# A row transform cut into two 64-row halves, in a kernel that adds a spectral filter and a gated mixture of experts

## The chip, the cores and the metric

The kernel runs on one core of one Trainium2 chip. The metric is the device time of one execution in microseconds (us); lower is better. Engines are named as in the profile: PE is TensorE (PEld its weight loads), DVE VectorE, ACT ScalarE, POOL GpSimd, SP SyncE, which issues most DMAs.

## The reference

```python
x = A_x                                  # [1, 2048, 512] f32
xn = _layernorm(x, axis=-1)
X = rfft2(xn) * (w_r + 1j * w_i)         # over tokens (2048) and features (512)
a = irfft2(X, s=(2048, 512))
gates = softmax(xn @ wg)                 # 8 experts, all 8 used: cw = gates / sum(gates)
h = gelu(einsum("nd,edf->nef", xn, w1))  # f = 1792
b = einsum("ne,ned->nd", cw, einsum("nef,efd->ned", h, w2))
return x + a + b
```

## The kernel before, in words

Nearly all of the time is the mixture of experts. Its two products are done in 32-bit floats split into a high and a low part (`split`: ACT writes the high part, DVE or POOL the low part), so each product is three passes of matmuls (`PASSES`). After a first slice that is done plainly (`mm1`, line 503, and `mm2`, line 525), the rest runs by a scheme of seven products for a two-by-two block (line 931), from about 155 us to the end.

The forward transform of the filter stands in the first stage, between those plain products. The 2048 tokens are 16 groups of 128, group b holding the tokens 16a + b. For each group, in the order `SEQ`:

- `folds` (POOL): sums and differences of the two halves of the feature axis, into `v`.
- `take_u`: `split` of `v` into `u`. `store_u` stores one half of `u` to DRAM as the table T3 of the later scheme, for groups 8 to 15.
- `over_d` (PE, line 360): the transform over features, two outputs p = 0 (even frequencies) and p = 1 (odd), of 268 and 264 columns. Their last 8 columns are the gate logits, for which `gate_tables` put `wg` beside the tables.
- `take_d`: the result becomes `X`, high part by ACT (line 372), low part by DVE (line 376); the gate columns are added into `lg` (lines 378, 380).
- `negate` (ACT, line 384): writes the negated real part behind the imaginary one, so that one matmul reads (real, imaginary) or (imaginary, minus real).
- `over_a` (PE, line 394): the transform over the 128 tokens of the group, 12 matmuls of 128 rows, 128 weight columns and 260 or 256 columns, from tables `mb` that `load_mb` and `split_mb` bring in.
- `take_a` (ACT) copies the result to `ys`, `store_a` (SP) stores it, one DMA for each p.

What runs when is written out by hand. The first stage is 28 blocks of 12 plain matmuls; around each block two numbered slots of `phase_a` are run, 56 in all. Slot 2n comes right behind block n in PE's order, then the ACT and DVE work on the block's result (`hidden`), then slot 2n + 1. `FFT` gives the slot of each group, `LAG` the distance of its steps, `RANK` the order within a slot; `MEANS`, `ROWS`, `SUMS`, `GATES`, `SPREAD` place the rest. `FIRST` is the order of the start, before block 0: loads, layer norm of the first four groups, their transposes (line 228), and matmuls on idle data (`fill`, `fill_rows`) that keep TensorE active. Every engine works in its order. PSUM has eight banks: two for `p1` (blocks of `mm1`, and the gate transposes of `spread`, line 320), four for `psf` (transposes and transforms), two for `p2` (`mm2`).

When a group of four token groups is through `take_d`, `softmax` makes the gates on DVE and ACT, `spread` transposes them and stores them to `cwd`, and `weights_of` reads them back.

## Time and profile before

| | us |
|---|---|
| median of 3 runs | 2265.36 (2263.53 to 2266.42) |
| the profiled execution | 2264.42 |
| its span, first to last instruction | 2262.6 |
| outside the span (2264.42 - 2262.6) | 1.8 |
| stretch with the forward transform | 22 to 135 |

The profile is one execution: the times of single instructions come from it, the medians from others. Instructions on TensorE are pipelined: a matmul's record is longer than the distance to the next one's start, so the net time of a block is read from start to start.

### The profile page before, as it was taken

Reading aid. Unit: us, or ns where it says so; the run is one execution under the profiler, and the core shown is the slowest. Engines: PE = TensorE matmul, PEld = TensorE weight load, DVE = VectorE, ACT = ScalarE, POOL = GpSimd, SP = SyncE. Lnnn points to the kernel's source line nnn. Section 1 sums busy time; section 2 is a strip of 40 time slices with the busy share of each in tenths; the row PEclk is TensorE's granted clock in tenths of the full one; section 3 lists DMA queues with packets and bytes.
Section 4 is the critical chain, followed back from the end, with each engine's and each line's share of the span. In section 5 each row is a group of like instructions: output and inputs, shape, how many; then the busy total and the mean of one; then the engine's idle time right before and its main releaser. Section 6 shows DMA issues by size and latency. Waiting matters only on the chain.

```text
span 2262.6 us, 27515 instructions
## 1 busy us (share of the span) xinstructions
PE 2249.3 (99%) x10271; PEld 1872.0 (83%) x10271; DVE 1891.8 (84%) x1823; ACT 1164.4 (51%) x1559; POOL 961.6 (42%) x660
## 2 busy tenths in 40 slices
PE   9999999999999999999999999999999999999999
PEld 8877888888888888888888888888888888888887
DVE  7758788888888888888878898888898888888776
ACT  7855455445455545545554545454554545455452
POOL 4216353455354544434344444445454434444340
PEclk9999999999999999999999999999999999999999
DMA  5788767677666666666677667766666666766663
GB/s 190 245 274 286 295 231 300 241 286 262 250 237 235 230 249 242 239 247 240 251 259 256 231 224 256 261 244 239 234 232 246 234 246 231 273 228 249 239 237 133
DMA packets 111686, 553.31 MB, mean 245 GB/s; under 512 B 11905, under 2 KB 22273, under 8 KB 55585
## 3 DMA queue, kind: packets, MB, share of 16 engines
q1 hardware_dynamic: 98816, 482.42, 58.5%
q10 hardware_dynamic: 11872, 64.94, 8.0%
q0 software_dynamic: 864, 4.19, 1.0%
q8 instruction: 82, 1.34, 0.2%
q14 instruction: 52, 0.42, 0.1%
HBM read 528.34 MB, written 29.98 MB: 247 GB/s over the span
## 4 chain that ended last, share of the span: by engine, by line
PE 96%; DMA 2%; ACT 1%; DVE 1%; issue 0%; SPq 0%; POOL 0%; ACTq 0%; DVEq 0%
PE pq L931 45%; PE pz L931 45%; PE p L525 1%; PE p L503 1%; PE pq L863 1%; PE psf L360 1%; PE psf L394 1%; DMA xr<-xs_b 1%; PE pq L876 0%; DMA xs_T<-d 0%; DMA mf<-in_mb 0%; DMA cwt<-cwd 0%; DMA acc<-in_x 0%; PE psf L228 0%; DMA cwd<-c 0%
## 5 line engine op out<-in xcount | busy, mean ns | idle before, releaser
L931 PE MATMUL pq<-xr,us 128*128 128x512 f32 x2580 | 619.9, 389 | 0.4 <-issue 0.4
L931 PE MATMUL pz<-hs,vs 128*128 128x512 f32 x2562 | 616.2, 389 | 0.0
L931 PEld LDWEIGHTS pq<-xr,us 128*128 128x128 f32 x2580 | 484.1, 188 | 101.8 <-issue 0.8
L931 PEld LDWEIGHTS pz<-hs,vs 128*128 128x128 f32 x2562 | 479.8, 188 | 99.2
L931 PE MATMUL pz<-hs,va 128*128 128x512 f32 x1974 | 473.7, 389 | 0.0
L931 PE MATMUL pq<-xr,ua 128*128 128x512 f32 x1932 | 464.3, 389 | 1.6 <-DMA xr<-xs_b 1.1
L931 PEld LDWEIGHTS pz<-hs,va 128*128 128x128 f32 x1974 | 369.4, 188 | 75.7
L931 PEld LDWEIGHTS pq<-xr,ua 128*128 128x128 f32 x1932 | 362.5, 188 | 77.7 <-DMA xr<-xs_b 1.6
L188 ACT CAST hs<-c 128x1024 fp32r<-128x1024 f32 x213 | 223.1, 1047 | 368.8 <-DVE c L1041 306.0
L1057 DVE TENSOR_TENSOR acc<-pz,acc 128x1024 f32<-128x1024 f32 x318 | 386.4, 1215 | 29.8 <-PE pz L931 28.5
L191 DVE TENSOR_TENSOR hs<-c,hs 128x1024 fp32r<-128x1024 f32 x213 | 302.5, 1420 | 78.9 <-ACT hs L188 78.9
L191 POOL TENSOR_TENSOR va<-raw,va 128x512 fp32r<-128x512 f32 x81 | 126.4, 1560 | 488.2 <-ACT va L188 477.6
L191 POOL TENSOR_TENSOR ua<-raw,ua 128x512 fp32r<-128x512 f32 x78 | 136.5, 1750 | 277.9 <-ACT ua L188 277.9
L1022 DVE TENSOR_TENSOR hs<-c,hs 128x1024 fp32r<-128x1024 f32 x162 | 211.5, 1305 | 48.9 <-ACT hs L1025 48.9
L1025 ACT CAST hs<-c 128x1024 fp32r<-128x1024 f32 x162 | 170.7, 1053 | 120.5 <-PE pz L931 64.3
L965 DVE TENSOR_TENSOR c<-pq,cwb 128x1024 f32<-128x1024 f32 x162 | 197.1, 1217 | 3.1 <-ACT pq L990 3.1
L191 POOL TENSOR_TENSOR us<-raw,us 128x512 fp32r<-128x512 f32 x52 | 73.4, 1411 | 184.1 <-ACT us L188 184.1
L996 ACT ACTIVATE c<-c 128x1024 f32<-128x1024 f32 x54 | 57.3, 1061 | 160.7 <-DVE c L995 160.7
L191 POOL TENSOR_TENSOR vs<-raw,vs 128x512 fp32r<-128x512 f32 x55 | 78.2, 1421 | 111.9 <-ACT vs L188 111.9
L995 DVE TENSOR_TENSOR c<-pq,c 128x1024 f32<-128x1024 f32 x54 | 66.1, 1224 | 64.3 <-PE pq L931 64.3
L1001 ACT ACTIVATE pq<-pq 128x1024 f32<-128x1024 f32 x54 | 54.4, 1008 | 125.2 <-DVE pq L1000 125.2
L1000 DVE TENSOR_TENSOR pq<-pq,c 128x1024 f32<-128x1024 f32 x54 | 66.5, 1232 | 62.1 <-PE pq L931 62.1
(185 smaller groups left out, 2448.5 us busy)
## 6 DMA issues: line engine op xcount, KB each, us to landing
xr<-xs_T SPq DMA_DIRECT2D x215, 1024.0 KB, 4.8
xr<-xs_b SPq DMA_DIRECT2D x161, 1024.0 KB, 4.8
cwb<-cwd SPq DMA_DIRECT2D x124, 256.0 KB, 5.3
raw<-in_wb ACTq DMA_DIRECT2D x27, 1024.0 KB, 4.9
raw<-in_wa ACTq DMA_DIRECT2D x26, 1024.0 KB, 5.0
xr<-cbd SPq DMA_DIRECT2D x32, 384.0 KB, 5.2
xs_b<-x SPq DMA_DIRECT2D x6, 1024.0 KB, 5.9
xs_T<-d SPq DMA_DIRECT2D x12, 512.0 KB, 4.9
```

Of the source, the lines that this page charges most:

```text
L188: nc.scalar.copy(dst[:, 0], src)
L191: (eng or nc.vector).tensor_tensor(dst[:, 1], src, r32(dst[:, 0]), op=ALU.subtract)
L360: nc.tensor.matmul(px, u[:, p, hu, k, :], fds[p][:, h, k, :R2], start=(n == 0), stop=(n == 5))
L931: nc.tensor.matmul(pt[:, m, :], w[:, hw, k, m * P : (m + 1) * P], x[:, hx, k, :], start=(start and n == 0), stop=(n == 5), skip_group_chec ...
L965: nc.vector.tensor_mul(dst, src, g)
L995: nc.vector.tensor_add(self.h22, self.X, self.h22)
L996: nc.scalar.activation(self.h22, self.h22, AF.Gelu_apprx_tanh)
L1000: nc.vector.tensor_add(self.X, self.X, self.u2)
L1001: nc.scalar.activation(self.X, self.X, AF.Gelu_apprx_tanh)
L1022: (nc.vector if self.u else eng(LOW["u0"][k - 4])).tensor_tensor(t[:, 1], h, r32(t[:, 0]), op=ALU.subtract)
L1025: nc.scalar.copy(t[:, 0], h)
L1057: nc.vector.tensor_add(to, self.z[(0, 1, 0, 1, 4, 4, 5)[k]], to)
```

## The change

The transform over the 128 tokens of a group is done as its first step says it can be: the sum and the difference of the two halves of 64 tokens, then a transform of 64 on each, which give the even and the odd frequencies. `folds` takes sum and difference on POOL (two more instructions for each group, a new tile `w`), so rows 0 to 63 of what `over_d` writes carry the sums and rows 64 to 127 the differences. `over_a` then runs pairs of matmuls of 64 rows, one on the upper and one on the lower half of the array, into two PSUM banks; real and imaginary part of the output lie in the two halves of the 128 weight columns, and one matmul covers both p (258 columns). `negate` and `store_u` go: the sign is in the table `mb` (192 instead of 256 columns), and T3 is split from `w` in `folds`, with two tiles `d` that `sums` uses too. `take_d` writes both p into one tile `X`. `store_a` issues four DMAs for a group instead of two, each of 64 partitions. The gate logits come out as sums and differences, so `softmax` first multiplies them by a table `pair` on TensorE, through a `p1` bank. `fill_rows` changes from 12 matmuls of 64 rows and 256 columns to 4 of the whole array and 16 of 64 rows, all of 128 columns. In `FIRST` one `fill` of a single matmul goes and one of two becomes one of one; the scale of group 3 moves from ACT to DVE, a weight's low part from DVE to POOL. Slots, ranks and engines of other steps are set anew, among them the moments of two token groups from slot 0 to slots 2 and 3, and the gate transposes of the first four groups from slot 17 to 15.

```diff
-XC = 144
+XC = 272
-XB = 2
+XB = 1
-MEANS = (0, 0, 0, 0, 8, 9, 5, 5, 29, 25, 27, 28)
+MEANS = (0, 0, 3, 2, 8, 9, 5, 5, 29, 25, 27, 28)
-SPREAD = ((17, 17), (26, 28), (41, 41), (50, 52))
+SPREAD = ((17, 15), (26, 30), (41, 41), (50, 52))
-SCALES = (0, 0, 0, 1)
+SCALES = (0, 0, 0, 0)
...
-    a = np.arange(P)
+    a, h = np.arange(P), np.arange(P // 2)
     m, cb = [], []
     for b in range(NB):
-        th = 2 * np.pi * (((16 * a[:, None] + b) * a[None, :]) % S) / S
-        m.append(np.concatenate([np.cos(th), np.sin(th)], 1))
-        th = th.T
+        th = [2 * np.pi * (((16 * h[:, None] + b) * (2 * h[None, :] + q)) % S) / S for q in range(2)]
+        th = np.concatenate(th, 0)
+        m.append(np.concatenate([np.sin(th), np.cos(th), -np.sin(th)], 1))
+        th = 2 * np.pi * (((16 * a[None, :] + b) * BINS[:, None]) % S) / S
         cb.append(_hl(np.concatenate([-np.sin(th), np.cos(th), np.sin(th)], 1)))
     out["mb"] = np.stack(m)
+    one = np.eye(H)
+    out["pair"] = np.block([[one, one], [one, -one]])
...
     def folds(b):
         g, n = divmod(b, 4)
         a = ags[g][:, :, :, n * P : (n + 1) * P]
+        w = fa.tile([P, 2, 2, P], F32, name="w")
+        nc.gpsimd.tensor_tensor(w[:, 0], a[:, 1], a[:, 0], op=ALU.add)
+        nc.gpsimd.tensor_tensor(w[:, 1], a[:, 1], a[:, 0], op=ALU.subtract)
         v = vs[b] = fa.tile([P, 2, 2, P], F32, name="v", bufs=VB)
-        nc.gpsimd.tensor_tensor(v[:, 0], a[:, 1], a[:, 0], op=ALU.add)
-        nc.gpsimd.tensor_tensor(v[:, 1], a[:, 1], a[:, 0], op=ALU.subtract)
+        nc.gpsimd.tensor_tensor(v[:, :, :, :H], w[:, :, :, :H], w[:, :, :, H:], op=ALU.add)
+        nc.gpsimd.tensor_tensor(v[:, :, :, H:], w[:, :, :, :H], w[:, :, :, H:], op=ALU.subtract)
+        if b >= 8:
+            i, c = divmod(b - 8, 4)
+            t3 = fa.tile([P, 2, TB], F32R, name="d", bufs=2)[:, 0].rearrange("p (h k t) -> p h k t", h=2, k=2)
+            split(t3, w[:, 1], eng(LOW["t3"]))
+            nc.sync.dma_start(xs["T3"][i][:, :, :, c * P : (c + 1) * P], r32(t3))
     def take_u(b):
         u = us[b] = fa.tile([P, 2, 2, 2, P], F32R, name="u", bufs=2)
         split(u.rearrange("p s h k t -> p h s k t"), vs.pop(b), eng(LOW["u"]))
-
-    def store_u(b):
-        if b >= 8:
-            i, c = divmod(b - 8, 4)
-            nc.sync.dma_start(xs["T3"][i][:, :, :, c * P : (c + 1) * P], r32(us[b][:, 1]))
...
     def softmax(t):
-        c = lgs.pop(t)
+        lg = lgs.pop(t)
+        c = xp.tile([P, 4, E], F32, name="sm")
+        pl = ps1.tile([P, TB], F32, name="p1")[:, : 4 * E].rearrange("p (j e) -> p j e", e=E)
+        nc.tensor.matmul(pl, pair, lg, start=True, stop=True)
         mx = xp.tile([P, 16], F32, name="mx", bufs=2)[:, :4]
-        nc.vector.tensor_reduce(mx, c, axis=AX.X, op=ALU.max)
-        nc.vector.tensor_sub(c, c, mx[:, :, None].to_broadcast([P, 4, E]))
+        nc.vector.tensor_reduce(mx, pl, axis=AX.X, op=ALU.max)
+        nc.vector.tensor_sub(c, pl, mx[:, :, None].to_broadcast([P, 4, E]))
...
     def load_mb(b):
-        mbf[b] = fa.tile([P, 2, P], F32, name="mf", bufs=MFB)
-        nc.sync.dma_start(mbf[b], io["mb"][b].rearrange("p (c a) -> p c a", c=2))
+        mbf[b] = fa.tile([P, 3 * H], F32, name="mf", bufs=MFB)
+        nc.sync.dma_start(mbf[b], io["mb"][b])
     def split_mb(b):
-        mbs[b] = fa.tile([P, 2, 2, P], F32R, name="mb", bufs=2)
+        mbs[b] = fa.tile([P, 2, 3 * H], F32R, name="mb", bufs=2)
         split(mbs[b], mbf.pop(b), eng(LOW["mb"]))
...
         lg = lgs[t][:, j]
+        X = Xs[b] = fa.tile([P, 2, 2, XC], F32R, name="X", bufs=XB)
         for p in range(2):
-            R = ROW[p]
-            Xs[b, p] = fa.tile([P, 2, 3, XC], F32R, name="X", bufs=XB)[:, :, :, :R]
-            px = pxs[b, p][:, : 2 * R].rearrange("p (c r) -> p c r", c=2)
-            nc.scalar.copy(Xs[b, p][:, 0, :2], px)
+            px = pxs[b, p][:, : 2 * ROW[p]].rearrange("p (c r) -> p c r", c=2)
+            nc.scalar.copy(X[:, 0, :, AT[p] : AT[p + 1]], px)
         for p in range(2):
             px = pxs.pop((b, p))
             R2 = 2 * ROW[p]
-            nc.vector.tensor_sub(Xs[b, p][:, 1, :2], px[:, :R2].rearrange("p (c r) -> p c r", c=2), r32(Xs[b, p][:, 0, :2]))
+            sl = slice(AT[p], AT[p + 1])
+            nc.vector.tensor_sub(X[:, 1, :, sl], px[:, :R2].rearrange("p (c r) -> p c r", c=2), r32(X[:, 0, :, sl]))
             if p:
                 nc.vector.tensor_add(lg, lg, px[:, R2:])
             else:
                 (nc.vector.tensor_copy if LOW['lg'] else nc.scalar.copy)(lg, px[:, R2:])
-    def negate(b):
+    def over_a(b):
+        mb, X = mbs.pop(b), Xs.pop(b)
+        py = pys[b] = [psf.tile([P, 512], F32, name="psf")[:, : AT[2]] for _ in range(2)]
+        n = 0
+        for c in range(2):
+            for h, hx in PASSES:
+                for q in range(2):
+                    rows = slice(q * H, q * H + H)
+                    nc.tensor.matmul(
+                        py[q], mb[rows, h, (1 - c) * H : (3 - c) * H], X[rows, hx, c, : AT[2]], start=(n == 0), stop=(n == 5)
+                    )
+                n += 1
+
+    yss = {}
+
+    def take_a(b):
+        st = yss[b] = fa.tile([P, 2, AT[2]], F32, name="ys", bufs=2)
+        for q, py in enumerate(pys.pop(b)):
+            nc.scalar.copy(st[:, q], py)
+
+    def store_a(b):
+        st = yss.pop(b)
         for p in range(2):
-            nc.scalar.mul(Xs[b, p][:, :, 2], r32(Xs[b, p][:, :, 0]), -1.0)
-
-    def over_a(b):
-        mb = mbs.pop(b)
-        for p in range(2):
-            X = Xs.pop((b, p))
-            py = pys[b, p] = psf.tile([P, 512], F32, name="psf")[:, : 2 * ROW[p]]
-            n = 0
             for c in range(2):
-                for h, hx in PASSES:
-                    nc.tensor.matmul(py, mb[:, h, c], X[:, hx, c : c + 2], start=(n == 0), stop=(n == 5))
-                    n += 1
-
-    yss = {}
-
-    def take_a(b):
-        for p in range(2):
-            st = yss[b, p] = fa.tile([P, 2, ROW[p]], F32, name=f"ys{p}", bufs=2)
-            nc.scalar.copy(st, pys.pop((b, p)).rearrange("p (c r) -> p c r", c=2))
-
-    def store_a(b):
-        for p in range(2):
-            nc.sync.dma_start(yd[p][b // 4][:, b % 4], yss.pop((b, p)))
+                to = yd[p][b // 4][:, b % 4, c].rearrange("(q k) r -> k q r", q=2)
+                nc.sync.dma_start(to, st[c * H : c * H + H, :, AT[p] : AT[p + 1]])
...
     def fill_rows(n):
         two = [pt, ps1.tile([P, TB], F32, name="p1")]
+        for _ in range(4):
+            nc.tensor.matmul(pt[:, :P], warm, warm, start=True, stop=True)
         for _ in range(n):
             for h in range(2):
                 rows = warm[64 * h : 64 * h + 64]
-                nc.tensor.matmul(
-                    two[h][:, : 2 * P].rearrange("p (n c) -> p n c", n=2), rows, rows[:, None].to_broadcast([64, 2, P]),
-                    start=True, stop=True,
-                )
+                nc.tensor.matmul(two[h][:, :P], rows, rows, start=True, stop=True)
...
-        fill_rows(6)
+        fill_rows(8)
+    ri = ri[BINS]
```

## Rows read from the trace of the kernel before

**Rows 1.** The page: the span, the busy time of each engine with its share of the span and its instructions.

```profile
span 2262.6 us, 27515 instructions
...
PE 2249.3 (99%) x10271; PEld 1872.0 (83%) x10271; DVE 1891.8 (84%) x1823; ACT 1164.4 (51%) x1559; POOL 961.6 (42%) x660
```

**Rows 2.** Busy time of each engine by stage: the stretch in us from the start of the span, its length, then busy us and instruction count of PE, PEld, DVE, ACT and POOL, the granted clock, the share of the DMA engines and GB/s.

```profile
0.00:25.00 25.00, 20.93 (x121) 17.34 (x122) 20.12 (x43) 16.43 (x36) 12.31 (x26) 1.00 0.80 285
25.00:135.00 110.00, 109.50 (x681) 97.75 (x680) 83.51 (x195) 86.58 (x203) 30.26 (x38) 1.00 0.66 209
135.00:160.00 25.00, 22.14 (x97) 17.20 (x96) 14.31 (x26) 13.65 (x25) 3.19 (x4) 1.00 0.94 303
160.00:2262.60 2102.60, 2096.71 (x9377) 1739.69 (x9375) 1773.84 (x1562) 1047.77 (x1297) 915.81 (x592) 1.00 0.67 245
```

**Rows 3.** Who TensorE waited for, in three stretches one after the other (0 to 30, 30 to 135 and 135 to 210 us): us in total, times, longest.

```profile
PE p L503 <- DVE w L490: 0.8, 2, 0.4
PE p L228 <- ACT u L217: 0.7, 1, 0.7
...
PE psf L394 <- ACT X L384: 0.5, 1, 0.5
...
PE pq L931 <- DVE raw L569: 2.6, 1, 2.6
PE pq L931 <- DMA xr<-xs_b: 1.1, 1, 1.1
```

**Rows 4.** The chain of work that ended last, its first and its last block of line 394: start us, us, what. Each piece is counted to the start of the next, so a block of twelve matmuls appears with its net time. After it, the instructions of line 394 as a whole (ns minimum/median/maximum, first and last start, forms).

```profile
28.08 1.44 PE psf L394 x12
...
133.53 1.43 PE psf L394 x12
...
L394 PEld LDWEIGHTS psf<-X,mb x192: 186/188/193, 27.8 to 134.6; 128*128 128x128 f32 x192
L394 PE MATMUL psf<-X,mb x192: 275/283/387, 27.9 to 134.7; 128*128 128x260 f32 x96, 128*128 128x256 f32 x96
```

**Rows 5.** The warm-up before. First the eleven matmuls of 512 columns on the whole array (line 635: ns minimum/median/maximum, first and last start us), then, in order of time and from narrow windows (each shows what overlaps it), the matmuls of 64 rows and 256 columns behind them, two halves in turn, and weight loads of these.

```profile
L635 PE MATMUL p<-x x11: 628/628/792, 1.5 to 5.9; 128*128 128x512 f32 x11
...
6.47 0.58 PE L644 MATMUL p<-x 64*128 64x256 f32 x2
...
6.85 0.44 PE L644 MATMUL p<-x 64*128 64x256 f32 x4
...
7.13 0.19 PEld L644 LDWEIGHTS p<-x 64*128 64x128 f32 x2
...
7.25 0.19 PEld L644 LDWEIGHTS p<-x 64*128 64x128 f32 x2
```

**Rows 6.** Line 503 between 18 and 24 us: the matmuls of 512 columns (ns minimum/median/maximum), the longest of them those that follow a wait.

```profile
L503 PE MATMUL p<-x,w x17: 283/393/499, 17.8 to 24.0; 128*128 128x512 f32 x14, 128*128 128x256 f32 x3
```

**Rows 7.** TensorE in order of time from 56 to 61 us: a block of line 360, four transposes of 128 columns (line 320), a product.

```profile
56.18 1.62 PE L360 MATMUL psf<-fd,u 128*128 128x268 f32 x12
57.64 0.60 PE L320 MATMUL p<-ident,cw 128*8 128x128 f32 x4
58.00 3.00 PE L503 MATMUL p<-x,w 128*128 128x512 f32 x12
```

**Rows 8.** Groups of ScalarE and then of VectorE between 25 and 135 us, shapes apart: busy us, mean ns of one, idle time before them and what ended it.

```profile
L384 ACT ACTIVATE X<-X 128x260 fp32r<-128x260 f32 x16 | 6.9, 432 | 1.9 <-DVE X L376 1.2 <-DVE mb L191 0.6
L384 ACT ACTIVATE X<-X 128x256 fp32r<-128x256 f32 x16 | 6.7, 419 | 0.0
L188 ACT CAST mb<-mf 128x256 fp32r<-128x256 f32 x15 | 6.2, 415 | 3.9 <-DMA mf<-in_mb 3.9
L188 ACT CAST d<-ag 128x512 fp32r<-128x512 f32 x10 | 6.0, 626 | 2.1 <-DMA xs_T<-d 2.1
...
L191 DVE TENSOR_TENSOR mb<-mf,mb 128x256 fp32r<-128x256 f32 x15 | 6.3, 421 | 2.9 <-ACT mb L188 2.8
```

**Rows 9.** GpSimd folds of line 255 (ns minimum/median/maximum) and, from the order of time, VectorE and GpSimd in the first 21 us: the start of the moments of two token groups, and two low parts of weights while GpSimd folds.

```profile
L255 POOL TENSOR_TENSOR v<-ag x12: 740/752/1003, 31.8 to 117.3; 128x256 f32<-128x256 f32 x12
...
13.77 0.68 DVE L205 BATCH_NORM_STATS2 st<-acc 128x6 f32<-128x512 f32 x1
...
14.58 0.66 DVE L205 BATCH_NORM_STATS2 st<-acc 128x6 f32<-128x512 f32 x1
...
19.11 1.83 DVE L490 TENSOR_TENSOR w<-raw,w 128x256 fp32r<-128x256 f32 x2
...
18.85 0.93 POOL L255 TENSOR_TENSOR v<-acc 128x256 f32<-128x256 f32 x1
```

**Rows 10.** ScalarE in order of time from 56 us: the first instruction after the product that ends at 56.3, and the copy that frees the PSUM buffer of the gate transposes.

```profile
56.54 0.60 ACT L515 ACTIVATE c<-p 128x512 f32<-128x512 f32 x1
...
58.54 0.57 ACT L323 COPY c<-p 8x512 f32<-8x512 f32 x1
```

**Rows 11.** TensorE and VectorE in order of time: the product that runs from 42.15 us, and the last gate sum of the first four token groups.

```profile
42.15 2.95 PE L525 MATMUL p<-h,w 128*128 128x512 f32 x12
...
43.79 0.15 DVE L378 TENSOR_TENSOR lg<-lg,psf 128x8 f32<-128x8 f32 x1
```

**Rows 12.** What the DMA queue of SyncE waited for between 25 and 135 us (us in total, times, longest), and the stores of line 406 as a whole (ns of issue).

```profile
SPq L346 <- DVE mb L191: 36.0, 12, 4.4
...
L406 SPq DMA_DIRECT2D yd<-ys x32: 319/540/1482, 29.2 to 137.9; - x32
```

45 lines of the change are left out of this document (25 added, 20 removed).

## The prediction

> **What bounds the kernel now.** I read the page first: TensorE is busy for 99% of a span of 2262.6 us, VectorE for 84% [rows 1]. That is a mean over stages, so next the busy times by stage [rows 2]. The change touches the first 155 us or so. In the stretch 25 to 135 us, where the forward transform runs, TensorE works 109.5 of 110 us, ScalarE 86.6, VectorE 83.5, GpSimd 30.3. Its waits, third, say the same from the other side [rows 3]: between 30 and 135 us it waits once, 0.5 us, for the negation on line 384. So in this stretch time taken off TensorE is time gained, as long as the other engines keep up. Outside it there are two places with gaps. Before 25 us it is idle for 25 - 20.9 = 4.1 us [rows 2], 0.8 of it in two waits for low parts of weights (line 490), and around 155 us it waits 2.6 us at line 931 [rows 3]. The work behind that second gap starts from the gate transposes that TensorE itself makes in slot 50, so the gap moves with TensorE and I leave it as it is.
>
> **What the change does, part by part.**
>
> *The halves.* Fourth, the chain of waits: a block of line 394 is 12 matmuls in 1.44 us net, the first as the last [rows 4], so 0.120 us each, and with 192 of them 16 blocks and 23.0 us. The new block has again 12 matmuls of 128 weight columns and about as many streamed (258 for 260 and 256), but of 64 rows, in pairs. What a pair costs the trace shows before the change, in the warm-up [rows 5]: there matmuls of 64 rows and 256 columns are issued to the two halves in turn; two loads start at 7.13 us, two at 7.25. A pair takes 0.12 us, what one matmul of 128 rows took. So a block becomes 6 x 0.12 = 0.72 us, and 16 blocks save 11.5 us. If the halves did not run together, nothing would be saved; that is a rival below.
>
> *Going over and back.* Each block stands between matmuls of the whole array, so there are 32 changes between the two forms. Rows 5 show one, while 512 columns still took (5.9 - 1.5) / 10 = 0.44 us, that is with the clock at its lower level of 1.2 GHz. The last whole-array matmul starts at 5.9 us and would be followed at 6.34; the first pair starts at 6.47, 0.13 later. The next pair starts at 6.85, 0.38 behind it, where 256 columns take half of 0.44, 0.22: 0.16 more, the load that could not be hidden behind a running matmul. Together 0.29 at the lower level. At the upper level the load has a price of its own: a matmul after a wait has a record of up to 0.499 us where the median is 0.393 [rows 6], 0.10 more. For the emptying I halve the 0.13 with the clock. That makes 0.165, and 32 x 0.165 = 5.3 us. Bounds: the load alone, 3.2; everything as at the lower level, 9.3. The Trainium skill has the rule: "TensorEngine Tiling (Array Packing)", Key Properties, says that changing the tiling mode drains TensorE, and gives no figure. The 0.13 us agrees with it; by a free change the net gain of this part would be 11.5, by the drain as taken it is 6.2.
>
> *The gate product.* Four matmuls of `pair` with 32 columns in full f32, which the trace of before does not show. The nearest rows are the transposes of 128 columns in f32: four in 0.36 us, from 57.64 to 58.00 [rows 7], 0.09 each. Below, one of these, 0.09; above, all four for one product, 0.36, and a load not hidden, 0.10. I take 0.2, so 0.8 in all (0.4 to 1.8). It waits for the last gate sum of its four groups. For the first four this is done at 43.9 us while a product runs from 42.15 to 44.9 [rows 11], so TensorE need not wait; VectorE, in turn, must now wait for TensorE, about 1 us four times, with its other work queued behind the maximum of line 306.
>
> *The gate transposes of the first four groups.* They take one of the two `p1` banks, now in slot 15, before block 8. Block 8 takes the other, and block 9 needs the first back. It is freed by the copy on line 323, still in slot 17, behind block 8's own gelu and split on ScalarE. Before, block 9 needed only that gelu. The copy ran from 58.54 to 59.1 us, with the gelu at 56.54 right after the product's end [rows 10], while TensorE goes from 56.18 with a transform of about 1.46 us to 57.64 and could start block 9 then [rows 7]: 1.4 us too early. ScalarE's order there is little changed, so I take 1.2 (0 to 1.5).
>
> *The start.* Two moments go from slot 0 to slots 2 and 3, each 0.81 us of VectorE from start to start (13.77 to 14.58) [rows 9], ahead of the two low parts that TensorE waits for at 20 and 21 us. These took 0.95 us each instead of 0.42 (the other low parts of that size, `mb` [rows 8]), while GpSimd was folding [rows 9]. Between the two waits' 0.8 us and the load after each, 1.0 can be won; the 0.7 at the fourth group's transposes [rows 3] I leave, since its scale now queues on VectorE. But GpSimd now folds twice as long there (a fold of 0.75 us, four for a group instead of two [rows 9]). I take -1.0 (-1.3 to +1.0).
>
> *Edits costed at nothing, and their cover.* ScalarE loses 32 negations, 13.6 us, and gains eight high parts for T3 of 0.41 us (the size of `mb`, 0.415 [rows 8]), 3.3 us. VectorE gains eight low parts of 0.42, 3.4 us, and loses a quarter of `mb`, 1.6. GpSimd gains 32 folds of 0.75 us, 24 us on 30. VectorE's instructions beside a fold can be long, as the two above by 0.5 us; I give it 4 us for that. Sum on VectorE: 83.5 + 3.4 - 1.6 + 4 = 89 us of about 105. TensorE covers this, with 16 us to spare; without that cover it is a rival. T3's copies wait on ScalarE for GpSimd, 1.5 us where a fold stands in the slot of its `keep_x` (once), and for `d`, where ScalarE already waits 2.1 us for stores [rows 8]; the freed 10 us cover it. SyncE issues 64 stores instead of 32, 0.54 us each [rows 12], some 17 us more; queued behind them are the loads of `mf`, which wait 36.0 us for their one buffer anyway [rows 12]. The idle-data matmuls of the start stand in TensorE's gaps. `X` in one tile frees as late as the later of its two predecessors did.
>
> **Sum.** -11.5 + 5.3 + 0.8 + 1.2 - 1.0 = -5.2 us. Against the profiled execution, 2264.4: 2259.2. The median of the runs is 0.9 higher, within their 2.9 us, and I leave the 2259.2. A measurement of this kernel tells a change from none from about 0.2% on, 4.5 us.
>
> **Rivals.**
>
> *Dear changes.* At the price of the lower level, 0.29, the sum is -11.5 + 9.3 + 0.8 + 1.2 - 1.0 = -1.2: 2263.2, no change. For it: emptying the array may not halve with the clock. Against: the load's price did nearly (0.16 to 0.10). *Cheap changes*, the load alone and no wait for `p1`: -11.5 + 3.2 + 0.8 - 1.0 = -8.5, 2255.9.
>
> *VectorE becomes the bound.* From 89 of 105 us in the mean it takes only a few places where its work comes in bunches. It decides from the point where TensorE waits 0.7 us more for each of eight groups: 5 us, so -0.2, 2264.2. For it: the new wait for the gate product and twice the folding. Against: the one wait in this stretch [rows 3] was for ScalarE, not VectorE.
>
> *The halves do not run together,* the other side. Twelve loads of 128 columns stay twelve; if one load sets the pace, a block stays at 1.44 us, and the changes come on top: +5.3 + 0.8 + 1.2 - 1.0 = +6.3, 2270.7, slower. It decides from a pair that takes 0.21 us: then the block saves 0.18 us, 2.9 in all, and the rest eats it. For it: the loads' records of 0.19 us exceed the pace of 0.12. Against it: the loads of rows 5 start two at a time. By the Trainium skill, "TensorE: Matmul & The Clock Gate", LDWEIGHTS (loading the stationary operand), a load takes time by its columns and not its rows, which alone would give this rival; the trace agrees as far as a load of 64 rows has the record of one of 128, but shows two at once.
>
> *The clock.* With two idle-data matmuls fewer between 8.7 and 12.4 us the clock could fall to its lower level, where a matmul takes 0.44 for 0.23 us. Over the 7 us of products behind, this costs up to 6, of which the start's gaps hide some: about -5.2 + 4 = -1.2, 2263.2. The granted clock of before is 1.00 in every stage [rows 2].
>
> **How the numbers follow.** Chances: the forecast 0.46; dear changes 0.16; cheap ones 0.16; VectorE 0.11; not together 0.08; the clock 0.03. The forecast counts as faster but for some 0.07 near the bound: faster 0.39 + 0.16 = 0.55. Slower: 0.08, and 0.02 from VectorE. The rest, 0.35, is no change. The range goes from the cheap changes with a better start (-10.5) to the cases around no change and a little over (+2.1): 2254 to 2266.5; what it leaves out is the halves apart and the ends of the other cases.
>
> **What would show it.** In the profile after: blocks of 12 matmuls of 64 rows in about 0.9 us, starting two at a time, with gaps of some 0.1 us ahead of and behind them; four short products of `pair`; a wait of block 9 for line 323; line 490's waits gone; TensorE at line 931 some 5 us sooner. It is wrong if pairs start 0.2 us apart, if the gaps come near 0.3, if TensorE shows waits for VectorE of more than 2 us in the stage, or if line 931 starts sooner and the end does not.

## The result, and the profile after

The changed kernel takes 2283.03 us in the median of four runs (2277.25 to 2285.18), the kernel before 2264.55 beside it: a ratio of 1.0077, 95% interval 1.0056 to 1.0098. It is 18 us slower, outside the predicted range and on the other side of no change. The profiled execution took 2285.18 us, with a span of 2283.4, 20.8 more than before [rows 1].

First the page of the changed kernel, its span and the busy times:

```profile
span 2283.4 us, 27591 instructions
...
PE 2255.0 (99%) x10285; PEld 1869.0 (82%) x10285; DVE 1901.9 (83%) x1835; ACT 1154.3 (51%) x1534; POOL 991.7 (43%) x689
```

Then the busy times by stage, columns as in rows 2:

```profile
0.00:25.00 25.00, 20.86 (x122) 18.02 (x123) 19.44 (x39) 15.02 (x33) 14.06 (x28) 0.93 0.76 278
25.00:135.00 110.00, 98.51 (x616) 80.89 (x615) 87.39 (x187) 71.01 (x165) 58.59 (x67) 0.97 0.61 172
135.00:160.00 25.00, 24.16 (x133) 19.51 (x132) 17.12 (x35) 14.56 (x29) 3.04 (x3) 1.00 0.89 248
160.00:2283.40 2123.40, 2111.49 (x9420) 1750.55 (x9418) 1777.91 (x1576) 1053.72 (x1309) 916.04 (x592) 1.00 0.67 245
```

Between 25 and 135 us TensorE was busy for 109.5 of 110 us [rows 2]; now it is for 98.5, at a mean clock of 0.97, with VectorE at 87.4 (the prediction had 89) and GpSimd at 58.6 for 30.3. Who TensorE waited for, between 30 and 135 and then between 135 and 210 us, tells more than the sums, since before there was one wait of 0.5 us in the first stretch [rows 3]:

```profile
PE psf L403 <- DVE x L256: 3.4, 2, 3.1
PE psf L235 <- DVE xn L226: 2.5, 3, 1.2
PE psf L403 <- DVE lg L393: 2.3, 1, 2.3
PE psf L235 <- ACT ys L413: 1.0, 1, 1.0
...
PE pq L945 <- DVE raw L584: 5.1, 1, 5.1
```

All but one of these name VectorE. Matching the same plain matmul in both traces, the changed kernel is late by 0.6 us at 12 us (times of the kernel before), 2.7 at 70, 9.8 at 91, 13.0 at 140, 15.3 at 155, and 20.9 from 207 us on, and by no more to the end: all of it is lost in the first tenth of the span. Part of it is the clock. Four stretches of the changed kernel, with the same columns:

```profile
8.90:12.30 3.40, 3.17 (x14) 2.99 (x15) 3.27 (x7) 2.32 (x6) 3.20 (x6) 0.52 1.03 415
97.70:104.50 6.80, 5.40 (x20) 4.40 (x21) 4.83 (x12) 4.14 (x11) 4.41 (x6) 0.51 0.75 262
169.40:176.20 6.80, 5.63 (x13) 4.46 (x14) 3.04 (x5) 1.27 (x3) 0.00 (x0) 0.50 1.02 426
224.00:227.40 3.40, 3.40 (x10) 2.67 (x9) 3.40 (x3) 1.32 (x2) 2.95 (x2) 0.51 0.01 5
```

The granted clock is about 0.5 there, the lower of the two levels; before it was 1.00 in every stage [rows 2], though that mean doesn't show the first 6 us, where 512 columns took 0.44 us [rows 5]. TensorE is busy for 17.6 us in these stretches, of which the full clock would have needed half, so up to 8.8 of the 20.8 us are the price of the clock. The last three begin in TensorE's waits of 3.1, 5.1 and 2.0 us, or right behind them. Not every such wait is followed so: behind that of 2.3 us, which ends at 78 us, the clock stayed at 1.00, and so it did in the kernel before behind one of 2.6 us. The second stretch, in order of time (start, us, and the idle time before in brackets):

```profile
99.10 1.66 PE L403 MATMUL psf<-X,mb 64*128 64x258 f32 x11 [3.15 <-DVE x L256]
100.68 4.83 PE L540 MATMUL p<-h,w 128*128 128x512 f32 x12
```

The product behind the wait takes 4.77 us to the next start (105.45) where the other products of line 540 take about 3: this wait of 3.1 us cost some 1.8 more behind it. What VectorE was late with is read one engine further, on ScalarE and then VectorE:

```profile
97.48 0.35 ACT L195 CAST mb<-mf 128x192 fp32r<-128x192 f32 x1 [5.49 <-DMA mf<-in_mb]
97.87 0.36 DVE L198 TENSOR_TENSOR mb<-mf,mb 128x192 fp32r<-128x192 f32 x1 [4.42 <-ACT mb L195]
```

So VectorE itself stood for 4.4 us, at the low part of a table `mb` whose load, issued by SyncE at 89.39 us, came 8 us later; `take_lo` (line 256), whose PSUM bank TensorE needed, stood behind it. SyncE issued the load as soon as its one buffer was free, and 0.9 us behind a load of 1 MB that GpSimd had issued:

```profile
88.48 1.07 POOL L558 DMA_DIRECT2D acc<-in_xt  x1
89.39 0.33 SPq L359 DMA_DIRECT2D mf<-in_mb  x1
```

Both landed between 97.2 and 97.5 us, while in the median a load of `mf` lands 2.4 us after its issue. SyncE's stores of `ys` stand behind it (from 89.77). In the kernel before the two loads were issued together (83.95 and 83.99 us), and the small one had landed by 86.43. So the one buffer puts this load where the large one holds it up; the second half of that is read from the landing times, and no run was made for it.

The waits of 2.3 and 5.1 us have the same look. A little before each, VectorE had stood for a load of gate weights from `cwd`, for 3.0 and 4.0 us:

```profile
72.19 1.67 DVE L555 TENSOR_TENSOR acc<-acc,v 128x1024 f32<-128x1024 f32 x1 [2.97 <-DMA v<-cwd]
...
162.84 0.33 SPq L551 DMA_DIRECT2D cwt<-cwd  x1
...
168.05 0.69 DVE L696 TENSOR_TENSOR acc<-p,cwt 128x512 f32<-128x512 f32 x1 [4.02 <-DMA cwt<-cwd]
```

In the kernel before VectorE waits for no load from `cwd` in this time. The load at 162.84 was issued 7.6 us after ScalarE's store of these gates; before, this took 4.0. Runs below move load and wait together for `mf` and for `cwt`; for `v` it is read from the order of time alone.

Then the queue that the prediction had costed at nothing. What SyncE waited for at the sends of T3 between 20 and 160 us, in the changed kernel (line 271) and, the last line, in the one before (line 265):

```profile
SPq L271 <- DVE d L198: 14.1, 5, 5.3
SPq L271 <- DVE sm L326: 2.5, 1, 2.5
SPq L271 <- DVE sm L320: 1.8, 1, 1.8
SPq L271 <- DVE ag L289: 1.3, 1, 1.3
```

```profile
SPq L265 <- DVE ag L283: 0.4, 1, 0.4
```

Before, `store_u` sent T3 four slots after the folds, when it was long there: 0.4 us of waiting. Now `folds` sends it in its own slot, and SyncE stands for 19.7 us, with the loads behind it. None of the three late loads above stands behind such a send. Where it shows in this trace is at the longest, the send of 110.80 us: behind it `v` is asked for at 117.52 us (101.04 before, some 5 of that more than the kernel is late there anyway), and VectorE stands 1.2 us for it.

### The profile page after: what moved, and what is told of

The parts are those of the page before. It is cut to its first block, busy times and chain, and to the rows that moved or that the text cites. A ratio compares the mean times of both kernels' runs of the same rounds, so it can differ in the third digit from the quotient of the medians.

```text
span 2283.4 us, 27591 instructions
## 1 busy us (share of the span) xinstructions
PE 2255.0 (99%) x10285; PEld 1869.0 (82%) x10285; DVE 1901.9 (83%) x1835; ACT 1154.3 (51%) x1534; POOL 991.7 (43%) x689
## 4 chain that ended last, share of the span: by engine, by line
PE 93%; DVE 3%; DMA 2%; ACT 1%; issue 0%; SPq 0%; POOL 0%; DVEq 0%; ACTq 0%; POOLq 0%
PE pz L945 45%; PE pq L945 44%; PE pq L877 1%; PE p L540 1%; PE p L518 1%; DMA acc<-in_xt 1%; PE pq L890 0%; DMA acc<-in_x 0%; PE psf L403 0%; DMA mf<-in_mb 0%; PE psf L373 0%; DVE u L198 0%; DMA cwt<-cwd 0%; SPq L420 0%; DVE x L256 0%
```

## The experiments

Theories: that the new slots are badly laid out; that the halves cost more than they save; that VectorE's total work is now the bound; and that single edits, each thought covered, make others late (the second folds, T3's split or its send, the stores, the one buffer `mf`). Times are medians in us; "before" is the kernel before in the same session.

| run | median | before | ratio (95%) |
|---|---|---|---|
| arith_only | 2282.44 | 2265.20 | 1.0076 (1.0061 to 1.0091) |
| h_only | 2264.53 | 2264.88 | 1.0000 (0.9990 to 1.0009) |
| h_folds | 2269.61 | 2264.88 | 1.0021 (1.0011 to 1.0030) |
| h_t3 | 2271.17 | 2264.88 | 1.0025 (1.0016 to 1.0034) |
| h_store4 | 2267.83 | 2264.88 | 1.0008 (0.9999 to 1.0017) |
| h_gate | 2265.41 | 2265.72 | 0.9997 (0.9987 to 1.0006) |
| b_interleave | 2265.83 | 2265.72 | 1.0001 (0.9991 to 1.0011) |
| b_folds2 | 2271.89 | 2265.20 | 1.0029 (1.0018 to 1.0041) |
| mf2 | 2279.77 | 2265.20 | 1.0062 (1.0047 to 1.0077) |
| one_store | 2280.52 | 2265.20 | 1.0061 (1.0044 to 1.0078) |
| store_mf | 2274.01 | 2265.72 | 1.0038 (1.0023 to 1.0053) |
| rescue_new | 2291.98 | 2265.72 | 1.0113 (1.0093 to 1.0133) |
| relief2 | 2280.14 | 2265.01 | 1.0066 (1.0051 to 1.0081) |
| sm_t3late | 2282.03 | 2265.01 | 1.0076 (1.0061 to 1.0091) |
| sm_nf_late | 2276.43 | 2265.01 | 1.0046 (1.0030 to 1.0063) |
| h_t3_late | 2275.19 | 2265.01 | 1.0045 (1.0030 to 1.0060) |
| h_t3_own_late | 2273.35 | 2265.06 | 1.0038 (1.0024 to 1.0052) |
| h_t3_own_sent | 2266.13 | 2265.06 | 1.0005 (0.9996 to 1.0015) |

### The layout: arith_only

The changed arithmetic with the start, slots, ranks and engines of the kernel before.

```diff
-FFT = (2, 4, 7, 9, 11, 14, 16, 18, 21, 25, 27, 30, 34, 37, 41, 43)
+FFT = (2, 4, 7, 9, 11, 14, 16, 18, 20, 25, 27, 31, 34, 37, 41, 43)
-MEANS = (0, 0, 3, 2, 8, 9, 5, 5, 29, 25, 27, 28)
+MEANS = (0, 0, 0, 0, 8, 9, 5, 5, 29, 25, 27, 28)
...
```

> The changed arithmetic (halves, folds, gate product, stores) with every slot, rank, engine choice and the whole start of the kernel before. Theory G (the doubled folds keep GpSimd busy, VectorE's instructions beside it grow, and late VectorE work holds PSUM banks back from TensorE): the loss stays, 2275 to 2285 us. Theory S (the loads of mf come late behind the smaller stores): the loss stays too. Theory L (the loss is in the new slots): it goes, 2256 to 2262 us. In any case the start has the clock of before, and block 0 begins within 0.2 us of 12.42.

2282.44, as the changed kernel (2283.03). The layout is not the cause, and the prediction's -1.0 for the start isn't seen in these medians either; the arithmetic and its side work are what costs.

### The halves, and one edit at a time on top

The base, h_only, is arith_only with the halves alone: two folds instead of four (so what is transformed is not the sums and differences), no product with `pair`, T3 sent from `u` as before, two stores a group.

```diff
-        w = fa.tile([P, 2, 2, P], F32, name="w")
-        nc.gpsimd.tensor_tensor(w[:, 0], a[:, 1], a[:, 0], op=ALU.add)
...
+        nc.gpsimd.tensor_tensor(v[:, 0], a[:, 1], a[:, 0], op=ALU.add)
+        nc.gpsimd.tensor_tensor(v[:, 1], a[:, 1], a[:, 0], op=ALU.subtract)
...
-        nc.tensor.matmul(pl, pair, lg, start=True, stop=True)
```

> The halves alone, on the old slots and the old start: over_a in pairs of 64 rows, the small table, one X tile, no negation. Left out are the sums and differences of token halves, the gate product and the split of T3 from w (T3 is stored from u as before); two stores for a group, of 128 partitions. Read before: 16 blocks of 0.94 us for 1.44 save 8.0 us. If the halves bring nothing else, 2257 us (-8, within 2); theory B (both PSUM banks of a group's pairs are needed at once, so TensorE waits for VectorE where one bank sufficed before) gives back 3 us or more even here: 2260 or later.

TensorE in order of time, the same three blocks in the kernel before and then in h_only:

```profile
39.23 1.63 PE L360 MATMUL psf<-fd,u 128*128 128x268 f32 x12
40.70 1.61 PE L394 MATMUL psf<-X,mb 128*128 128x260 f32 x12
42.15 2.95 PE L525 MATMUL p<-h,w 128*128 128x512 f32 x12
44.94 1.63 PE L360 MATMUL psf<-fd,u 128*128 128x268 f32 x12
```

```profile
40.05 1.62 PE L368 MATMUL psf<-fd,u 128*128 128x268 f32 x12
41.60 0.99 PE L398 MATMUL psf<-X,mb 64*128 64x258 f32 x12
42.52 3.06 PE L533 MATMUL p<-h,w 128*128 128x512 f32 x12
45.42 1.63 PE L368 MATMUL psf<-fd,u 128*128 128x268 f32 x12
```

From start to start that is 1.47 + 1.45 + 2.79 = 5.71 us before, and 1.55 + 0.92 + 2.90 = 5.37 with the halves. They do run together, and 0.34 us is saved, over 16 blocks 5.4. Yet the median is no lower. In the profiled execution, TensorE between 30 and 155 us now waits 1.5 us for `take_lo`, 1.4 for the copies of `ys`, 0.7 for a scale; the product behind the 1.5 takes 4.6 us at the lower clock (1.6 too many), and the clock was also at the lower level early in the start (1.2 us late at 12 us). That is 6.4 us, where 5.4 were won: TensorE was ahead of engines that had just kept up. By this count 2.8 of the 6.4 are the clock. Where the clock held, something was left: the profile of h_gate, the same kernel with the gate product, has 1.00 in all of the first 25 us and a span of 2261.3 us, 1.3 below that of before.

The four edits, each alone on h_only, in this order: the second folds (h_folds), T3's split and send in the folds' slot (h_t3, with the T3 of the first folds), four stores a group (h_store4), the gate product (h_gate).

```diff
+        w = fa.tile([P, 2, 2, P], F32, name="w")
...
+        nc.gpsimd.tensor_tensor(v[:, :, :, :H], w[:, :, :, :H], w[:, :, :, H:], op=ALU.add)
+        nc.gpsimd.tensor_tensor(v[:, :, :, H:], w[:, :, :, :H], w[:, :, :, H:], op=ALU.subtract)
```

```diff
+            split(t3, v[:, 1], eng(LOW["t3"]))
+            nc.sync.dma_start(xs["T3"][i][:, :, :, c * P : (c + 1) * P], r32(t3))
```

```diff
-            nc.sync.dma_start(yd[p][b // 4][:, b % 4], st[:, :, AT[p] : AT[p + 1]])
+            for c in range(2):
+                to = yd[p][b // 4][:, b % 4, c].rearrange("(q k) r -> k q r", q=2)
+                nc.sync.dma_start(to, st[c * H : c * H + H, :, AT[p] : AT[p + 1]])
```

```diff
+        nc.tensor.matmul(pl, pair, lg, start=True, stop=True)
```

> The halves alone and the second level of folds on GpSimd (two more instructions for a group). Theory G: it costs as much here as when the folds were doubled in the kernel before, 6.7 us, or up to twice that since TensorE leaves less time: 6 to 13 us above the halves alone. If the folds mattered only through the stretch before 25 us: 2.5 us above.

> The halves alone with T3 split on its own, eight more high parts on ScalarE and low parts on VectorE through the two tiles d, from the feature folds; no second folds, no gate product. Theory V (VectorE has no time left): 3 to 6 us above the halves alone. If ScalarE's freed time and VectorE's gaps cover it, as predicted: within 1 us.

> The halves alone with four stores for a group, of 64 partitions in pieces of 512 and 520 bytes, as changed. Theory S: mf comes late and the loads at 155 us land later, 3 to 6 us above the halves alone. Otherwise within 1 us.

> The halves alone with the gate product of pair on TensorE, through a p1 bank. As predicted 0.8 us for the products; with VectorE's waits for them up to 2 us more: 1 to 3 us above the halves alone (2264.5).

Over h_only the folds cost 5.1 us, T3 6.6, the stores 3.3 (this last is the least certain: its interval against the kernel before still touches none). h_gate is 0.3 below its own kernel before, h_only 0.35, so the gate product is nearly free: less than the 1 to 3 us expected, though 0.8 could not be told from nothing here. The sum of the four, -0.35 + 5.1 + 6.6 + 3.3 + 0.05 = 14.7 over the 2265.2 before, is 2279.9 against arith_only's 2282.4: nearly all of the loss, and additive to some 3 us.

Where the stores cost shows once in the profile of h_store4. The buffer of `mf` is free at 84.0 us, but SyncE is issuing the four stores until 85.1, so the load goes out at 85.21, 1.2 us behind the 1 MB load of 84.04, and lands 8.6 us later; ScalarE stands 6.8 us for it, and TensorE 3.7 us for a copy of ScalarE's behind that. In h_only the two loads go out together (85.93 and 85.96), the table is read at 88.14, and this wait isn't there.

How the folds cost shows in VectorE, GpSimd and TensorE in order of time at the start, h_only and then h_folds:

```profile
18.34 0.68 DVE L198 TENSOR_TENSOR fd<-d,fd 128x512 fp32r<-128x512 f32 x1
...
22.05 1.43 PE L511 MATMUL p<-x,w 128*128 128x512 f32 x5 [0.39 <-DVE w L498]
```

```profile
18.20 1.23 DVE L198 TENSOR_TENSOR fd<-d,fd 128x512 fp32r<-128x512 f32 x1
...
18.84 1.19 POOL L263 TENSOR_TENSOR w<-acc 128x256 f32<-128x256 f32 x1
...
22.64 1.76 PE L514 MATMUL p<-x,w 128*128 128x512 f32 x6 [1.99 <-DVE w L501]
```

The same low part takes 1.23 us beside a fold and 0.68 without, and TensorE waits 2.0 us for the weights behind it, where in h_only it waited 0.4 and, just before, 0.3. By form between 25 and 135 us, h_only and then h_folds (busy us, mean ns):

```profile
L198 DVE TENSOR_TENSOR u<-v,u 128x512 fp32r<-128x512 f32 x14 | 11.0, 784 | 0.6 <-ACT u L195 0.6
L256 DVE TENSOR_TENSOR x<-psf,x 128x512 fp32r<-128x512 f32 x12 | 8.2, 683 | 1.4 <-ACT ag L252 1.2
```

```profile
L198 DVE TENSOR_TENSOR u<-v,u 128x512 fp32r<-128x512 f32 x15 | 13.8, 919 | 1.5 <-ACT u L195 1.5
L256 DVE TENSOR_TENSOR x<-psf,x 128x512 fp32r<-128x512 f32 x12 | 8.2, 681 | 0.9 <-ACT ag L252 0.6
```

`u`, with both inputs in SBUF, goes from 784 to 919 ns; `x`, of the same size but with one input in PSUM, stays at 683 and 681. By the Trainium skill, "SBUF — State Buffer", Who interferes with whom, a VectorE instruction with two SBUF inputs contends with a GpSimd instruction that reads SBUF; the rows agree for these two. An instruction with one tensor and two columns of scalars, all in SBUF, is hit as well: `xn` (line 226) takes 543 ns alone and up to 947 beside a fold in h_folds.

The kernel before with its folds done twice puts the same cost without any halves:

```diff
+        for _ in range(2):
             nc.gpsimd.tensor_tensor(v[:, 0], a[:, 1], a[:, 0], op=ALU.add)
             nc.gpsimd.tensor_tensor(v[:, 1], a[:, 1], a[:, 0], op=ALU.subtract)
```

> The kernel before with the two folds of each group done twice on GpSimd, nothing else. Theory G: VectorE's instructions beside the folds grow by 3 to 6 us in all and TensorE waits more than the 0.5 us of before in 30 to 135 us: 2 to 6 us slower than the kernel before. Without it: within 1 us.

+6.7 us: some 23 us more on an engine with 80 to spare, costed at 4 us of VectorE's slack. And b_interleave, the kernel before with its two p taken in turn, so that both PSUM banks are filled at the same time, as with the halves:

```diff
-        for p in range(2):
...
         for c in range(2):
             for h, hx in PASSES:
+                for p in range(2):
+                    nc.tensor.matmul(py[p], mb[:, h, c], X[p][:, hx, c : c + 2], start=(n == 0), stop=(n == 5))
```

> The kernel before with the 12 matmuls of a group's token transform in the order p = 0, 1, 0, 1 instead of six and six: the same matmuls on the whole array, but both PSUM banks are wanted at the first of them and both come free after the last. Theory B (the halves' gain is lost to the banks, 4 of them for all transforms): TensorE waits for VectorE and ScalarE at transposes and transforms, 2 to 5 us slower than the kernel before. If the banks do not matter: within 1 us.

No difference: needing both banks at once costs nothing in the kernel before. (It wasn't tried on the changed one.)

### Stores, `mf`, and VectorE's total

On the changed kernel: a second tile `mf` (mf2), one store a group of 128 partitions (one_store), both (store_mf).

```diff
-MFB = 1
+MFB = 2
...
-        for p in range(2):
-            for c in range(2):
-                to = yd[p][b // 4][:, b % 4, c].rearrange("(q k) r -> k q r", q=2)
-                nc.sync.dma_start(to, st[c * H : c * H + H, :, AT[p] : AT[p + 1]])
+        nc.sync.dma_start(yd[b // 4][b % 4], st)
```

> The changed kernel with two mf buffers instead of one, the second filled at the start. Theory S: ScalarE's waits for mf (2.3 us at 74 us, 5.5 us at 92 us) go, and with them two waits of TensorE of 2.3 and 3.2 us and the clock's fall at 98 us: 8 us faster than the changed kernel, about 2275. Theory G: the waits move to other places, less than 3 us faster.

> The changed kernel with one store of 128 partitions and 2064 bytes each for a group instead of four of 64 partitions in pieces of 512 and 520 bytes; the later loads of Y take the pieces apart (16 loads instead of 8). Theory S, with SyncE's issue time as its cause (2.6 us and more for a group): mf is issued sooner, 4 to 8 us faster than the changed kernel. Theory G: within 3 us of it.

> The changed kernel with both: one store for a group and two mf buffers. If the two act on the same loss, as mf's late loads would have it, 3 us faster than the changed kernel, as each alone; if on different ones, 6 us, about 2276.

Against 2283.0 they gain 3.3, 2.5 and 9.0. The first two are within the spread of the runs, the third is clear of it, and it is the branch of two different losses in the expectation of store_mf. The traces show which. TensorE's two longest waits of after, 3.1 us behind `mf` and 5.1 us behind `cwt`, in mf2 and then in one_store:

```profile
PE psf L403 <- DVE x L256: 0.2, 1, 0.2
PE pq L945 <- DVE raw L584: 5.3, 1, 5.3
```

```profile
PE psf L403 <- DVE x L256: 3.0, 2, 2.8
PE pq L944 <- DVE raw L581: 2.7, 1, 2.7
```

The second buffer takes away the first wait and leaves the second; one store for four leaves the first (its load of `mf` still came 7.7 us after its issue, again behind the load of 1 MB) and halves the second, with the load of `cwt` issued 4.6 us after the gates' store instead of 7.6. In store_mf the first is 0.2 us, and the longest at that line is 2.3, for a load. So in the changed kernel it is `cwt` that the four stores make late, and not this load of `mf`: at 158 us (time of the kernel before) the changed kernel is 17.7 us late, mf2 11.8, one_store 14.5 and store_mf 6.8. In the medians mf2 shows less of it than its trace does.

Then work taken off VectorE, on store_mf: scales of 12 groups and shared copies to ScalarE (relief2), and the copies of the gate logits too (rescue_new, whose diff this is; relief2 keeps `'lg': 1`).

```diff
-            for name, fn in (("scale", scale), ...
+            for name, fn in (("scale", lambda b: scale(b, None, nc.scalar)), ...
-LOW = {'t3': 1, 'gates': 0, 'lg': 1, 'p2': (1, 0, 1, 0, 0, 0, 1, 0, 0, 0, 1, 1, 0, 0, 0, 1),
+LOW = {'t3': 1, 'gates': 0, 'lg': 0, 'p2': (0, 0, 0, 0, 0, 0, 0, 0, 0, 0, 0, 0, 0, 0, 0, 0),
...
```

> The changed kernel with one store, two mf buffers, and VectorE relieved at ScalarE's expense: the scaling of the 12 later groups, the copies of the plain products and the first gate columns move to ScalarE (about 12 us of VectorE's 87 between 25 and 135 us). Theory V (VectorE is the bound of the stage): TensorE's waits for VectorE go, 8 us or more faster than with one store and two buffers, 2260 to 2270. If VectorE only passes on what GpSimd and the banks hold up: within 3 us of it.

> The changed kernel with one store a group and two mf tiles (2274.0 us), and work taken off VectorE: the scaling of the 12 later groups and the copies of the products that were shared out to VectorE go to ScalarE, the gate's copy stays on VectorE. Complete. Theory VectorE is the bound (its row in the changed kernel: 87 of 110 us between 25 and 135, 21 of 21 between 25 and 46): some 8 us less work for VectorE there, 2266 to 2270. Theory order and waits: VectorE's total isn't the bound but the place where it and ScalarE wait in their order, so nothing is gained or ScalarE becomes the later one, 2273 to 2280.

Stage 25 to 135 us of store_mf and then of relief2:

```profile
25.00:135.00 110.00, 101.73 (x640) 83.71 (x638) 92.43 (x198) 72.68 (x171) 58.58 (x66) 0.98 0.63 193
```

```profile
25.00:135.00 110.00, 100.57 (x630) 82.37 (x630) 81.80 (x176) 81.44 (x183) 59.64 (x73) 0.98 0.60 182
```

VectorE has 10.6 us less to do there, and the kernel is 6.1 us slower. So the sum on VectorE alone is not what sets the time: what counts is when it gets to the one instruction TensorE waits for. The work went to ScalarE, which now has 81.4 us for 72.7, and part of TensorE's waits now name ScalarE; whether ScalarE has become the later engine, as the expectation allowed, this run doesn't separate. In rescue_new my move of `lg` made it worse in another way:

```profile
ACT lg L396 <- DVE X L392: 15.3, 15, 4.8
```

ScalarE, in its order, now waits for VectorE at the logits, 15 us in all.

### T3: its work, its place, its tiles or its send

T3's 6.6 us were the largest item, and in h_t3 ScalarE waited 6.4 us over four copies for the folds (line 263). My first theory was that wait, so the split was moved behind that of `u`, two slots later; on h_t3 (h_t3_late), on store_mf (sm_t3late), and there without the second folds (sm_nf_late).

```diff
             ("folds", folds), ("take_u", take_u),
+            ("t3_part", t3_part),
```

> The run with the halves and T3's split in the folds' own slot (2271.2 us; halves alone 2264.5), with the split moved behind the splitting of u in a slot two later, where the folds that it reads are long done; the same instructions, eight copies on ScalarE and eight differences on VectorE. The T3 sent is that of the first folds, so the output is not the transform, as in that run. Theory head-of-line: T3's 6.6 us is ScalarE standing in its fixed order behind the copy that waits for GpSimd's folds (6.4 us of waits over 4 copies in that run's trace) with everything queued behind it. Then 2264.5 to 2267.5, and no ScalarE wait of more than 0.5 us for the folds at line 263. Theory work: it is the time of the eight copies and differences themselves (about 0.6 + 0.7 us each) on engines that have no room; then 2269.5 to 2272, as with the split in the folds' slot.

> The changed kernel with one store a group and two mf tiles (2274.0 us), and T3's split moved behind the splitting of u in the same way (w has two tiles for it, v two in place of three). Complete: all outputs are computed. Theory head-of-line: 2268 to 2271. Theory work: 2272.5 to 2275.5.

> The run before this one without the second folds: u and T3 are formed from the first folds, so GpSimd does two folds a group as in the kernel before and the output is not the transform. The second folds cost 5.1 us on the halves alone. Theory head-of-line with a sum that adds up: 5 us less than the run before this one, 2263 to 2266, level with the kernel before within 0.1%. Theory that losses of the changed kernel are one common bound (VectorE's time) and do not add: 2268 or more.

The wait for the folds went, and the time rose, by 4.0 and 8.0 us: that theory fell. (The folds are worth 5.6 us here too, 2282.0 to 2276.4, with the tiles of `w` and `v` changed along with them.) The trace of h_t3_late showed what was late instead, on VectorE:

```profile
111.04 2.36 DVE L553 TENSOR_TENSOR acc<-acc,v 128x1024 f32<-128x1024 f32 x2 [3.66 <-DMA v<-cwd]
```

It waits for the broadcast weights `v`, and on SyncE, just ahead of that load, stands the send of T3 (line 274), waiting for VectorE's low part. With two tiles of T3's own (h_t3_own_late, the first pair of lines) and then also the send two slots later, where `store_u` had it (h_t3_own_sent, the second pair):

```diff
-            t3 = fa.tile([P, 2, TB], F32R, name="d", bufs=2)[:, 0].rearrange(...)
+            t3 = fa.tile([P, TB], F32R, name="t3", bufs=2).rearrange(...)
...
-            nc.sync.dma_start(xs["T3"][i][:, :, :, c * P : (c + 1) * P], r32(t3))
+            t3s[b] = t3
```

> The run with T3's split behind the splitting of u (2275.2 us; halves alone 2264.5), with two tiles of T3's own in place of the two that it shares with the twelve splits of T1, T2 and T4 (v has two tiles for three); the send still follows the split at once. T3 is that of the first folds. Theory tiles: the cost is ScalarE waiting for a tile whose send hasn't landed (7.7 us over 4 copies in that run's trace); then 2265 to 2269. Theory SyncE's order: the send stands in SyncE's queue right behind the split and waits there for VectorE's difference (10.6 us over 2 sends between 95 and 125 us), ahead of the loads of mf and of the broadcast weights v<-cwd, for which VectorE then stood 3.7 us with what TensorE needed behind it; then 2271 to 2276. Theory work: 2270 to 2275.

> The run beside this one (T3 split behind the splitting of u, into two tiles of its own) with the send moved two slots later, to where the halves alone send that part of u: all that is left of T3's edit against the halves alone is eight copies on ScalarE and eight differences on VectorE, and one tile of v less. T3 is that of the first folds. Theory SyncE's order, and theory tiles too: 2264.5 to 2267.5, and VectorE waits for v<-cwd less than 0.5 us. Theory work (eight copies and differences, about 0.4 us each on two engines): 2269 to 2275, wherever the send stands.

The tiles are worth 1.8 us at most (the runs of the two overlap), the place of the send 7.2 (2273.35 to 2266.13), and with both right T3's split costs 1.6 us over h_only, which is not clear of nothing. The 7.2 is for a split that already stands two slots behind the folds. In the changed kernel split and send stand in the folds' own slot, and there only both together were measured, 6.6 (h_t3); less the 1.6 that leaves some 5 us for the place, an estimate. SyncE's issues and VectorE in order of time around 110 us in h_t3_own_late, and then SyncE's in h_t3_own_sent:

```profile
110.10 0.52 SPq L274 DMA_DIRECT2D xs_T<-t  x1
110.71 0.57 SPq L549 DMA_DIRECT2D v<-cwd  x1
...
114.98 2.36 DVE L553 TENSOR_TENSOR acc<-acc,v 128x1024 f32<-128x1024 f32 x2 [2.32 <-DMA v<-cwd]
```

```profile
102.40 0.44 SPq L555 DMA_DIRECT2D v<-cwd  x1
...
108.61 0.52 SPq L274 DMA_DIRECT2D xs_T<-t  x1
```

`v` is asked for at 102.4 us when the send stands behind it, and at 110.7 when it stands ahead. Of these 8.3 us about 4 are the send's: the stores of `ys` just ahead of both are already 4.1 us later. In the kernel with the early send VectorE waits 2.3 us for `v`, with the low parts that TensorE needs queued behind; with the late one 0.3. A larger loss in the same trace comes earlier. Behind an early send SyncE asks for the 1 MB load of `raw` at 64.31 us instead of 62.80, the load of `mf` issued at 67.25 then lands only after 8.5 us, and TensorE waits 3.4 us at line 403:

```profile
75.78 0.35 ACT L195 CAST mb<-mf 128x192 fp32r<-128x192 f32 x1 [5.72 <-DMA mf<-in_mb]
```

So here too it is a load that comes late, for ScalarE and then VectorE.

## Why the prediction was wrong, point by point

- *The halves*: right. A pair runs together, and a block stands at 0.92 us from start to start, as forecast. If all 12 are at 0.06, the changes cost 5.37 - 5.71 + 0.72 = 0.38 us for two, 0.19 each where 0.165 was taken; net 5.4 for 6.2. The rival of halves apart, the only one that forecast slower, is excluded.
- *The gate product*: no error to be seen; 0.8 and nothing can't be told apart here. VectorE does wait for it, 2.2 us in three times in the changed kernel, and that too cost nothing that can be told from none.
- *Block 9's wait for a `p1` bank*: no such wait stands in the profile after; +1.2 was not needed.
- *The start*: no gain in the profiled execution, which is 0.6 us late at 12 us and 1.2 at 24, with the clock at the lower level from 8.9 to 12.3 us. The rival of the clock named the two idle-data matmuls fewer as its cause, but h_only has the old start and shows 0.93 in the first 25 us too, while store_mf has the new one and shows 1.00; what decides it is open. The low parts at line 505 still took 0.95 us, beside the folds, and TensorE still waits 1.1 us for them. Against arith_only, the old start with the doubled folds, 2.6 us late at 24 us, the new one is 1.4 us ahead, by one execution of each.
- *Edits costed at nothing, and their cover*: this is the step that failed, three times. The covers were sums over the stage (VectorE 89 of 105 us, ScalarE's freed 10, the 36 us that `mf` "waits anyway"), and TensorE doesn't wait for a sum. The second folds, given 4 us of VectorE's slack, cost 5.1 to 6.7 of the kernel's time. The four stores cost 3.3 on the halves, and together with the one `mf` 9.0 in the changed kernel; the cover, that the loads of `mf` wait for their buffer anyway, doesn't hold where a load that comes late makes TensorE wait, 3.1 us in the changed kernel and 3.7 in h_store4, and the load of `cwt` wasn't looked at. T3 cost 6.6. Its send has no term at all: the prediction counted its copies on ScalarE and its low parts, but not that its DMA was moved from four slots behind the folds into their slot, in SyncE's order ahead of the loads of `mf` and `v`; some 5 of the 6.6 us are this place, by the estimate above. In their place the runs show a sum of 15.0 us for these three, where the prediction has none: the folds make low parts longer, the stores and the send make loads later, and TensorE stands behind them.
- *VectorE becomes the bound*: the nearest rival in its signs (TensorE waiting for VectorE), priced at 5 us, but not in its mechanism: lightening VectorE by 10.6 us, at ScalarE's expense, made the kernel slower. Nor did any rival say that the clock can fall behind a wait in the middle of the stage; the clock is up to 8.8 us of the loss in the profiled execution.

What stays open: the send's place was moved on the halves alone; for the changed kernel that run, with memory for T3's own tiles, wasn't made. Its 19.7 us of waits on SyncE are no measure of the cost: store_mf stands even longer at these sends, 25.8 us, and is 9.0 us faster. Also open are the large loads in front of `mf`, which no run moved for themselves, and what decides whether the clock falls behind a wait. The best run that still computes everything is store_mf at 2274.0, 0.38% behind the kernel before; none beat that kernel, and of the 5.4 us that the halves save on TensorE none showed in a median.

## What to carry to other kernels

Where TensorE is busy for 99.5% of a stage, time taken off it is only worth what the other engines can follow: h_only saved 5.4 us there, and its median gave all of it back. A cover is not a sum of free time: for each edit ask which instruction that TensorE waits for stands behind it in which engine's order, the DMA queue's included, and read the issue and landing times of the loads in both traces. The three longest waits of TensorE in the changed kernel each came a little after another engine had stood for a load. Three edits "costed at nothing" cost 15 us.

## What the runs showed of the hardware

- Two matmuls of 64 rows on the two halves of the array run together in full: 12 of them with 258 columns take 0.92 us from start to start where 12 of 128 rows took 1.45. Going from one form to the other costs about 0.19 us, if all 12 stand at 0.06.
- VectorE's instructions with both inputs in SBUF take up to 1.23 instead of 0.68 us beside a GpSimd fold (128x512), and those with one input in PSUM don't (683 and 681 ns).
- Behind three of TensorE's waits in the changed kernel, of 3.1, 5.1 and 2.0 us, the granted clock was 0.5, and 12 matmuls behind them took 4.6 to 5.5 us for about 3. Behind a wait of 2.3 us in the same execution, and one of 2.6 in the kernel before, it stayed at 1.00; what decides it these runs don't show.
- A load of 96 KB landed 8.1 and 8.6 us after its issue where that stood 0.9 and 1.2 us behind the issue of a load of 1 MB (the changed kernel, h_store4). Issued within 0.1 us of the large one it was there after 2.4 at most (the kernel before, h_only).
